# A new order for all steps of a recurrent attention with a gated layer behind it, and a table load of the sine's own

## The chip, the cores and the metric

The kernel runs on one core of one Trainium2 chip. The metric is the time of one execution on the device, in microseconds. The engines, each with its own queue of instructions, are TensorE (PE in the profile; its weight loads are PEld), VectorE (DVE), ScalarE (ACT), GpSimd (POOL) and SyncE (SP), which issues nearly all DMAs.

## The reference, cut to what matters

```python
# q, k, v, f_logit: (4, 8, 768, 48)
f = 1.0 / (1.0 + np.exp(-f_logit))
for t in range(S):
    state = f[:, :, t, :, None] * state + np.einsum('bhd,bhe->bhde', k[:, :, t], v[:, :, t])
    y[:, :, t] = np.einsum('bhd,bhde->bhe', q[:, :, t], state)
x = y.transpose(0, 2, 1, 3).reshape(3072, 384)
h = x @ w_in                    # (384, 2048)
out = (h * np.cos(h)) @ w_out   # (2048, 384)
```

## The kernel before, in words

**Chunks.** The recurrence is turned into matrix products over chunks of 128 tokens. Two chunks make a *pair* of 256 tokens; a batch has three pairs, and there are twelve, 0 to 11. Pairs 0 and 1 have their loads and gates cut in two halves (`.0` and `.1`, four heads each); the others are loaded whole.

**The steps of a pair n.** Every step has a name, and the same names are used in the order of the work.
- `f`, `k`, `q`, `v` (lines 300 to 302, on SP): the loads.
- `ex`, `ln`, `fx`, `fy` (lines 333 to 351, ScalarE): the logarithm of the gate, and the gate itself. `ad` (line 367, GpSimd) adds the logarithms of neighbouring tokens. `cum` (lines 378 and 384, TensorE) sums them along the chunk; `eb` and `ei` (lines 395 and 399, ScalarE) are the exponentials of these sums, with either sign.
- `qa`, `ka` (lines 342, 345 and 355) fold one token's gate into q and k; `qm`, `km` (line 408) multiply by the decays. They read two operands in SBUF and may be put on VectorE or GpSimd.
- `tq`, `tk` (line 439) transpose on TensorE into PSUM and `qkt` (line 198) copies the result to SBUF; for pairs 5 to 11 a DMA transpose issued by SP (line 428) does both.
- `sc` (line 462, TensorE) are the scores, `am` (line 474, VectorE) masks them.
- `vb`, `vt` (line 198, GpSimd or ScalarE) cast and rearrange v.
- `ps` (line 492, TensorE) is the product that makes the state; `st`, `sd` (lines 504 and 509, VectorE) add the state carried and decay it; `sm` (lines 517 and 519) spreads it for the next product.
- `y`, `yi` (line 545, TensorE) sum the chunk's output in PSUM; `xe` (line 198) copies it to SBUF as x.

**The steps of a unit m.** The layer behind it runs over units of tokens: two of 128, then eleven of 256.
- `h` m.js (line 612, TensorE): x times a part of w_in; two halves s fill a PSUM place of two banks. In the two narrow units such a half has twelve matmuls, otherwise six.
- `co` (line 617, ScalarE): the cosine, as the sine with pi/2 added. `g` (line 584, VectorE): the product with h.
- `o` c.s (line 634, TensorE): chunk c of 128 tokens, one fourth of w_out each; `ot` copies the sum, `out` (line 646) stores it. The last chunk, 23, is cut in two columns, `a` and `b`.

**The weights.** `w0.i` and `w1.i` (line 286) load fourths of w_in and w_out, 768 KB each, into slots that g later uses; `wc` (line 198) casts them to bf16.

**The order.** `ORDER` is a text written by a planner outside the kernel. A word as `g0.0:V2` names the step, the letter of the engine (T, S, V, G, Y for TensorE, ScalarE, VectorE, GpSimd, SP) and the slot or PSUM bank of what it makes. `emit` issues the steps in just that order, and each engine works through its own in order. The waits follow from what the steps read and write. `zf` steps (line 268) are matmuls of zeros that nobody reads; they stand where TensorE would wait in the first part. `zsp`, `zqk`, `zvt` zero the edges of buffers once.

ScalarE's functions lie in two tables here: one for the exponential and the logarithm, one for the sine. `emit` asks for the first by an instruction (line 677) where a step of it follows one of the sine's; the load of the second is put in automatically and has the line of the sine, 617.

Of the kernel before, what the change touches and what calls it, by code (L numbers as in the profile page):

```python
# [55 lines left out]
h0.11:T0 co2.1:S2 h0.10:T qa2:G h1.11:T4 h1.10:T co2.0:S0 qm2.1:G0 g2.1:V3 wc1.0:G qm2.0:G co0.1:S1  # L56
v2:Y1 co1.1:S2 g2.0:V h2.20:T6 h2.21:T co2.2:S0 h2.31:T2 h2.30:T co2.3:S3 sm1.1:S0 wc1.1:G g0.1:V
g1.1:V g2.2:V o3.0:T0 o0.0:T1 o1.0:T4 tq2.1:T5 o3.1:T tq2.0:T6 o1.1:T f3:Y1 ka2:G km2.1:G
tk2.1:T w1.3:Y4 f4:Y0 v3:Y0 zsp.1:G g2.3:V km2.0:V wc1.2:S ex3:S ln3:S0 fx3:S zqk.2:G
tk2.0:T k3:Y0 vb2:G0 o3.2:T qkt2.1:V0 sc2.1:T2 vt2.1:G0 wc1.3:S vt2.3:G ps2.1:T5 ps2.0:T k4:Y1  # L60
o1.2:T qkt2.0:V1 st2.0:V o0.1:T sc2.0:T6 vt2.0:G q4:Y0 sd2.0:V0 o0.2:T am2.1:V0 sm2.0:G1 yi2:T5,2
ex4:S ln4:S1 vt2.2:G fx4:S ad3:G1 fy4:S ad4:G2 am2.0:V1 y2:T xe2.1:V0 xe2.0:V cum3:T3
o3.3:T o0.3:T ot3:V0 ot0:V1 vb3:G0 o1.3:T h3.20:T6 cum4:T2 eb3:S0 ot1:V2 f6:Y2 ei3:S0
ka3:V km3.0:V0 h3.01:T0 ei4:S1 eb4:S1 h3.00:T h3.21:T km3.1:V ps3.0:T2,3 ps3.1:T ka4:G h3.10:T4
sd3.0:V0 st3.1:V h3.11:T sd3.1:V1 qa4:G h3.31:T2 h3.30:T co3.2:S0 g3.2:V0 o4.2:T6 km4.0:G1 q3:Y1
qm4.0:G qm4.1:G q5:Y2 co3.0:S1 o2.3:T7 f5:Y0 v4:Y0 q6:Y0 sm3.1:S0 co3.1:S2 co3.3:S0 out3:Y
out0:Y g3.0:V tk4.0:T0 g3.1:V km4.1:G fy3:S g3.3:V o4.0:T tk3.0:T1 tq4.1:T4 tq4.0:T qkt4.0:V0
# [690 lines left out]
```

## Time and profile before

| what | value |
|---|---|
| time, median of 3 runs | 178.4 us (178.3 to 178.56) |
| time of the profiled execution | 179.66 us |
| its span | 177.4 us |
| granted TensorE clock | 1.00 |
| busy: PE, DVE, ACT, POOL | 170.8, 136.0, 137.7, 100.1 us |
| a load of f, k, q or v (whole) | 384 KB |
| loads of weights | 8 of 768 KB |
| HBM read, written | 25.17 MB, 4.72 MB |

Times of the profile count from the span's start. A row of the timeline gives start, duration, engine, line, operation, the tile written and those read, the count, and, where the engine had been idle, for how long and who ended that. A table of stretches gives the busy time and the count of each engine in each stretch. In the chain of waits a row is start, duration, and the work that the end depended on. "<-DMA" means that a load's landing ended the wait.

### The profile page before, as it was taken

The numbers are of one execution on the slowest core, as the hardware profiler recorded it, in microseconds if no ns is written. First come the engines' busy times: TensorE is split into PE (matmuls) and PEld (weight loads), VectorE is DVE, ScalarE is ACT, GpSimd is POOL, SyncE is SP. The second block draws the span as 40 slices with busy tenths as digits, with TensorE's granted clock in tenths as the row PEclk, the third lists the DMA queues.
The fourth block names the chain that finished last, engine by engine and source line by source line (L and its number), as shares of the span: only waits on it lengthen the run. The fifth ranks groups of instructions, "written<-read, shape, count | busy, mean of one in ns | idle before, by whom it ended". The sixth has DMA issues, their size and how long they took to land.

```text
span 177.4 us, 5843 instructions
## 1 busy us (share of the span) xinstructions
PE 170.8 (96%) x2470; PEld 124.8 (70%) x2470; DVE 136.0 (77%) x196; ACT 137.7 (78%) x205; POOL 100.1 (56%) x128
## 2 busy tenths in 40 slices
...
GB/s 127 276 261 306 353 352 351 305 229 280 256 258 286 285 185 134 285 171 235 247 260 279 211 227 232 199 155 163 48 193 2 0 137 4 0 44 4 0 113 198
DMA packets 72281, 33.92 MB, mean 191 GB/s; under 512 B 65344, under 2 KB 70720, under 8 KB 72256
## 3 DMA queue, kind: packets, MB, share of 16 engines
...
HBM read 25.17 MB, written 4.72 MB: 168 GB/s over the span
## 4 chain that ended last, share of the span: by engine, by line
PE 75%; DMA 11%; ACT 3%; DVE 3%; SPq 2%; POOL 2%; issue 1%; DVEq 0%; POOLq 0%
PE ps L634 33%; PE ps L612 28%; DMA g<-in_moe_w_in_dram 5%; DMA v<-in_v_dram 5%; PE ps L545 4%; PE ps L462 3%; SPq L286 2%; PE ps L492 2%; PE ps L268 2%; POOL w_in_bf L198 2%; DMA f<-in_f_logit_dram 2%; PE ps L439 1%; DVE am L474 1%; PE ps L378 1%; DVE qk L408 1%
## 5 line engine op out<-in xcount | busy, mean ns | idle before, releaser
L584 DVE TENSOR_TENSOR g<-ps,co 128x1024 bf16<-128x1024 f32 x48 | 60.1, 1309 | 19.2 <-ACT co L617 16.0
L634 PE MATMUL ps<-w_out_bf,g 128*128 128x384 bf16 (+1 forms) x400 | 69.2, 320 | 0.8 <-ACT w_out_bf L198 0.8
L612 PE MATMUL ps<-x,w_in_bf 128*128 128x256 bf16 (+1 forms) x624 | 66.6, 264 | 0.5 <-POOL w_in_bf L198 0.4
L617 ACT ACTIVATE co<-ps,halfpi 128x1024 bf16<-128x1024 f32 x48 | 51.7, 1113 | 18.2 <-PE ps L612 16.3
L612 PEld LDWEIGHTS <-w_in_bf 128*128 128x128 bf16 x624 | 56.5, 98 | 8.4 <-issue 0.6
L634 PEld LDWEIGHTS <-g 128*128 128x128 bf16 x400 | 37.1, 98 | 21.0 <-issue 1.0
L474 DVE TENSOR_TENSOR am<-ps,pmask 128x1024 bf16<-128x1024 f32 x22 | 26.0, 1216 | 1.5 <-PE ps L462 1.4
L408 POOL TENSOR_TENSOR qk<-q,b 128x384 bf16<-128x384 f32 x18 | 17.8, 1003 | 3.4 <-DVE q L342 2.2
L408 POOL TENSOR_TENSOR qk<-k,bi 128x384 bf16<-128x384 f32 x16 | 16.3, 1027 | 4.8 <-issue 2.0
L198 POOL COPY vt<-vb 64x384 bf16<-64x384 bf16 x31 | 15.3, 503 | 1.4
L268 PE MATMUL ps<-zero 128*128 128x512 bf16 x44 | 13.9, 426 | 1.2 <-DVE zero L204 1.2
L198 ACT COPY ot<-ps 128x384 f32<-128x384 f32 (+1 forms) x13 | 5.9, 450 | 8.9 <-PE ps L634 7.2
L198 POOL CAST vb<-v 128x768 bf16<-128x768 f32 x9 | 7.7, 861 | 8.3 <-DMA v<-in_v_dram 8.3
L333 ACT ACTIVATE f<-f 128x768 f32<-128x768 f32 (+1 forms) x14 | 10.3, 751 | 2.5 <-DMA f<-in_f_logit_dram 2.4
L198 DVE CAST x<-ps 128x384 bf16<-128x384 f32 x16 | 8.4, 550 | 4.5 <-PE ps L545 4.4
L519 POOL TENSOR_TENSOR sz<-sd,half 128x384 bf16<-128x384 bf16 x10 | 8.2, 826 | 5.8 <-DVE sd L509 5.5
L367 POOL TENSOR_TENSOR sp<-ls 128x384 bf16<-128x384 f32 x10 | 10.0, 1001 | 2.6 <-ACT ls L337 2.3
L345 POOL TENSOR_TENSOR q<-f,q 128x384 f32<-128x384 f32 x9 | 9.3, 1037 | 1.0 <-DMA q<-in_q_dram 0.4
L355 POOL TENSOR_TENSOR k<-k,f 128x384 f32<-128x384 f32 (+1 forms) x7 | 6.8, 973 | 4.1 <-DMA k<-in_k_dram 2.0
L198 DVE COPY ot<-ps 128x384 f32<-128x384 f32 (+1 forms) x13 | 6.7, 519 | 3.2 <-PE ps L634 3.0
L462 PE MATMUL ps<-qkt 48*64 48x128 bf16 (+1 forms) x304 | 8.9, 219 | 0.1
L198 ACT COPY vt<-vb 64x384 bf16<-64x384 bf16 x17 | 8.6, 508 | 0.3
...
## 6 DMA issues: line engine op xcount, KB each, us to landing
...
```

Source lines behind the costliest of these rows:

```text
L198: (nc.scalar.copy if e == "ACT" else eng(e).tensor_copy)(out=o, in_=i)
L268: G.step(f"zf{i}", ("PE",), lambda e, dump=dump: nc.tensor.matmul(dump.ap, lhsT=zero[:, 0:128], rhs=zero, start=True, stop=True), writes=[ ...
L333: nc.scalar.activation(out=flat(t.ap), in_=flat(t.ap), func=AF.Exp, scale=-1.0)
L345: eng(e).tensor_mul(out=w.ap[:, :, 0, :], in0=t.ap[:, :, 1, :], in1=w.ap[:, :, 0, :])
L367: G.step(f"ad{n}", ("POOL",), lambda e: eng(e).tensor_add(out=sp.ap[:, 0, :, 0:D], in0=soft.ap[:, :, 0, :], in1=soft.ap[:, :, 1, :]), read ...
L408: G.step(f"{nm}{n}.{u}", ("POOL", "DVE"), lambda e, u=u, j=j, src=src, dec=dec: eng(e).tensor_mul(out=qkp[u][j].ap[:, :, :, 0:D], in0=swap ...
L462: nc.tensor.matmul(o[t, r, 2 * a + g, :].rearrange("p (e n) -> p e n", e=2), lhsT=w, rhs=qkv(u)[s, 0, a, g, :, :], start=(a == 0 and g == ...
L474: G.step(f"am{n}.{u}", ("DVE",), lambda e, u=u, sc=sc: nc.vector.tensor_mul(out=am[u].ap.rearrange("p r b n -> p (r b) n"), in0=sc.ap.rear ...
L584: nc.vector.tensor_mul(out=o.rearrange("p b (n e) -> p b e n", e=2), in0=ph.ap.rearrange("p (b e n) -> p b e n", e=2, n=64), in1=co.ap.rea ...
L612: nc.tensor.matmul(ph.ap[:, i * T:(i + 1) * T].rearrange("p (g t) -> p g t", t=C), lhsT=w_in_bf[:, kk, f0:f0 + 128], rhs=xa[:, :, kk, :], ...
L617: G.step(f"co{m}.{j}", ("ACT",), lambda e, ph=ph, co=co: nc.scalar.activation(out=co.ap, in_=ph.ap, func=AF.Sin, bias=halfpi), reads=[ph], ...
L634: nc.tensor.matmul(po.ap[:, 0:c1 - c0], lhsT=gap[:, j, i * C:(i + 1) * C], rhs=w_out_bf[:, j, c0:c1], start=(po.first and j == 4 * s), sto ...
```

## The change: what it does

It changes three things.

1. `ORDER` is another text. All steps of pairs and units are the same, but their order, the engine of some, and the slots differ. Steps by engine, before and after: `ka` 7 on VectorE and 7 on GpSimd, then 3 and 11; `km` 8 and 16, then 6 and 18; `qm` 6 and 18, then 2 and 22; `qa` 5 and 9, then 4 and 10. `vt`: 31 on GpSimd and 17 on ScalarE, then 28 and 20. `wc`: 5 and 3, then 6 and 2. `xe`: 16 on VectorE and 8 on ScalarE, then 13 and 11. `ot`: 13 and 13, then 11 and 15. `qkt`: 9 and 1, then 8 and 2. `sm`: one moves from GpSimd to VectorE. Two stores, `out22.1` and `out23.0`, are issued by ScalarE.
2. The matmuls of zeros are 41 and no longer 44 (the width of each could now be set; all are 512 as before).
3. `emit` asks for the sine's table by an instruction too.

New code that cuts the loads and casts of w_in in halves is there, but `CUT_LOAD` and `CUT_CAST` are empty, so it does nothing; `SC8` isn't used.

The diff, with the order cut to the words around the first use of the weights:

```diff
+CUT_LOAD = ()
+CUT_CAST = ()
+SC8 = 1
-ZEROS = 44
+ZEROS = (512,) * 41
 ORDER = """
-zsp.2:G zvt.0:V f0.0:Y0 f0.1:Y ex0.0:S q0.1:Y0 k0.0:Y0 zqk.1:G q0.0:Y f1.1:Y1 ln0.0:S2 ex0.1:S
...
-q2:Y0 w1.0:Y4 qkt1.0:V1 ex2:S ln2:S0 xe0.1:S wc0.0:S zf39:T2 sc1.0:T4 zf40:T2 zf41:T2 yi1:T6,2
-ad2:G2 zf42:T3 zf43:T3 cum2:T3 vt1.1:G am1.1:V0 vt1.0:G fy2:S h0.00:T0 wc0.1:G am1.0:V1 w1.1:Y0
-fx2:S eb2:S0 y1:T st1.1:V xe1.0:V1 ei2:S1 xe1.1:S k2:Y1 sd1.1:V1 h1.00:T4 h2.00:T2 w1.2:Y1
-h0.01:T h1.01:T h2.11:T6 wc0.3:G zqk.0:G co0.0:S0 wc0.2:G g0.0:V2 h2.01:T h2.10:T co1.0:S1 g1.0:V
...
+zsp.1:G zqk.1:G f0.1:Y0 f0.0:Y ex0.1:S ex0.0:S ln0.1:S1 ln0.0:S q0.0:Y0 fx0.0:S qa0.0:V zvt.0:V
...
+ps1.0:T7,3 zf35:T4 tq1.1:T w0.3:Y3 xe0.1:S qkt1.1:V0 sd0.1:V0 ps1.1:T st1.0:V qm1.0:G ad2:G1 zf36:T4
+zf37:T4 zf38:T4 zf39:T4 tq1.0:T sc1.1:T0 sd1.0:V1 wc0.0:S k2:Y0 qkt1.0:S1 zf40:T4 cum2:T2 ei2:S1
+h1.00:T4 am1.1:V0 st1.1:V sc1.0:T0 am1.0:V1 sd1.1:V2 sm1.0:S0 eb2:S0 sm0.1:G1 wc0.1:G q2:Y1 vt1.3:G
+zqk.0:V h0.00:T6 h0.01:T co0.0:S0 w1.1:Y4 w1.3:Y1 y1:T0,1 v2:Y1 wc0.2:G w1.2:Y2 f4:Y1 yi1:T
+xe1.1:S1 h1.01:T xe1.0:V h0.10:T2 sm1.1:V0 co1.0:S1 h2.20:T0 g0.0:V0 wc0.3:G g1.0:V h2.21:T h0.11:T
+co2.2:S2 co0.1:S1 h1.10:T6 ka2:G km2.0:G0 qa2:G zsp.0:V qm2.1:G km2.1:G h1.11:T g2.2:V3 co1.1:S0
+g0.1:V h2.00:T4 g1.1:V h2.01:T co2.0:S2 h2.10:T0 h2.11:T wc1.1:S qm2.0:G h2.31:T2 tk2.1:T6 h2.30:T
+f3:Y0 g2.0:V tk2.0:T7 tq2.1:T qkt2.1:V0 co2.1:S0 o0.1:T4 tq2.0:T co2.3:S1 w1.0:Y4 wc1.3:G g2.1:V
+vb2:G0 vt2.1:G0 vt2.3:G vt2.2:G k3:Y0 o1.1:T5 g2.3:V qkt2.0:S1 o0.3:T o1.3:T sc2.0:T0 am2.0:V0
+sc2.1:T6 v3:Y0 ps2.1:T2 ps2.0:T st2.0:V sd2.0:V0 o3.3:T3 wc1.2:G ex4:S ln4:S0 vt2.0:G o3.1:T
+o1.2:T o0.2:T ex3:S ln3:S1 sm2.0:G1 yi2:T2,0 q4:Y0 am2.1:V1 y2:T xe2.1:V0 k4:Y1 v4:Y1
+ad4:G0 f6:Y2 cum4:T1 xe2.0:S o3.2:T ad3:G1 q3:Y1 fy3:S eb4:S0 ei4:S0 wc1.0:G h3.31:T6
+fx3:S fy4:S h3.30:T cum3:T2 eb3:S1 ei3:S1 ka3:V h3.21:T0 fx4:S km3.0:V0 vb3:S0 o0.0:T
+co3.3:S0 o1.0:T o3.0:T ot0:V0 ps3.0:T2,4 km3.1:G ps3.1:T ot3:V1 sd3.0:V0 qa4:G qm4.1:G1 st3.1:V
...
+co7.3:S1 g6.0:V g7.1:V g7.3:V cum9:T2 eb9:S1 vt9.0:S1 ka9:G vt7.2:G o11.1:T3 o12.2:T6 o11.0:T
+ei9:S0 o12.0:T o11.2:T sc7.1:T0 tq8.1:Y2 qm8.0:G zqk.2:V ps8.1:T7 am7.1:V0 sc7.0:T4 tq8.0:Y3 ex11:S
+vt8.3:S ex10:S am7.0:V1 vt8.1:G ln11:S0 vt7.3:S o12.3:T o10.2:T2 o12.1:T ps8.0:T st8.0:V sc8.0:T0
+am8.0:V2 sc8.1:T4 sd8.0:V0 ot12:S1 sm7.0:S2 vt8.2:G km9.0:G0 am8.1:V3 km9.1:G o10.1:T o11.3:T o10.0:T
+ot11:S2 ln10:S1 qm9.0:G y7:T0,1 sm8.0:G3 yi7:T ad10:G0 yi8:T3,4 y8:T fy11:S xe7.0:S0 xe8.0:S1
+xe8.1:V ps9.0:T0,5 ps9.1:T vt9.2:S out8:Y tq9.0:Y4 sc9.0:T6 o10.3:T xe7.1:V zsp.2:V sd9.0:V0 ot10:V0
...
 """
-        if s.table is not None:
-            if s.table == "E" and table != "E":
-                nc.scalar.preload_act_table_set("natural_log_exp_and_others")
+        if s.table is not None and s.table != table:
+            nc.scalar.preload_act_table_set({"E": "natural_log_exp_and_others", "S": "trig_and_small"}[s.table])
             table = s.table
```

More of the change, by code (lines that the diff above doesn't have):

```diff
@@ L56 @@
[L56 to L67, printed above, removed]
@@ L92 @@
-vt9.2:G vt8.2:G g6.0:V o12.0:T4 o10.1:T5 o12.3:T cum9:T0 o12.2:T ei9:S1 km9.0:G2 eb9:S1 qm9.0:G
-qm9.1:G km9.1:G vt7.1:G o12.1:T ps8.0:T0 ps8.1:T sc7.1:T6 st8.0:V sc8.0:T2 ex11:S sm7.1:S1 am8.0:V0
-sd8.0:V0 am7.1:V1 ot12:S1 tq7.0:Y2 o13.2:T1 o13.0:T ex10:S o13.1:T ln11:S0 o13.3:T fy11:S tq8.1:Y3
-out7:Y q10:Y0 sc7.0:T2 am7.0:V2 ps9.1:T0,4 vt8.1:G sc8.1:T6 ps9.0:T q11:Y1 am8.1:V3 ln10:S1 fy10:S
-sm8.0:S3 v11:Y0 k10:Y0 o10.3:T o10.2:T sd9.0:V0 ot13:V0 yi7:T2,3 y7:T xe7.1:S0 fx10:S vt8.0:G
-yi8:T6,7 vb10:G2 out12:Y ad10:G0 y8:T st9.1:V xe7.0:V ad11:G1 vt10.0:G1 cum10:T0 eb10:S0 sd9.1:V1
@@ new lines @@
+ot11:S2 ln10:S1 qm9.0:G y7:T0,1 sm8.0:G3 yi7:T ad10:G0 yi8:T3,4 y8:T fy11:S xe7.0:S0 xe8.0:S1
+xe8.1:V ps9.0:T0,5 ps9.1:T vt9.2:S out8:Y tq9.0:Y4 sc9.0:T6 o10.3:T xe7.1:V zsp.2:V sd9.0:V0 ot10:V0
+st9.1:V cum10:T4 sd9.1:V1 k11:Y0 k10:Y1 fx10:S ei10:S0 out6:Y am9.0:V0 fx11:S eb10:S0 h8.31:T0
+h8.21:T2 h8.30:T h8.20:T vt9.3:G qm9.1:G tq9.1:Y0 ad11:G1 o13.3:T4 o13.2:T o13.1:T o13.0:T co8.2:S0
+co8.3:S1 ot13:S3 fy10:S v11:Y0 q10:Y0 out13:Y vb10:G1 vt9.1:G g8.2:V1 ka10:G h8.00:T6 km10.0:G1
+km10.1:G sm9.1:S0 g8.3:V vb11:G0 ps10.1:T2,3 ps10.0:T sc9.1:T4 h8.01:T out12:Y vt10.2:S0 co8.0:S0 st10.0:V
```

149 lines of the change are left out of this document (78 added, 71 removed).

## The prediction

> **What bounds the kernel now.** I read the page's busy times and slices first, then a table of stretches, then the chain of waits, then the timeline of the stage that looked unlike the rest.
>
> ```profile
> PE 170.8 (96%) x2470; PEld 124.8 (70%) x2470; DVE 136.0 (77%) x196; ACT 137.7 (78%) x205; POOL 100.1 (56%) x128
> ...
> core 0: us, PE busy (x) PEld busy (x) DVE busy (x) ACT busy (x) POOL busy (x), PEclk, DMA share, GB/s
> 1.20:21.30 20.10, 19.52 (x269) 10.29 (x269) 15.88 (x46) 16.50 (x36) 8.37 (x15) 1.00 1.09 275
> 21.30:46.10 24.80, 23.31 (x333) 17.64 (x334) 18.30 (x22) 21.21 (x26) 19.19 (x22) 1.00 1.06 303
> 46.10:54.00 7.90, 7.73 (x98) 6.12 (x96) 7.11 (x11) 7.66 (x12) 6.75 (x8) 1.00 1.11 258
> 54.00:127.00 73.00, 72.98 (x1211) 55.86 (x1209) 65.61 (x89) 68.77 (x103) 62.66 (x78) 1.00 1.02 214
> 127.00:174.30 47.30, 47.28 (x567) 34.87 (x565) 28.79 (x30) 22.81 (x31) 2.57 (x4) 1.00 0.21 59
> 174.30:177.40 3.10, 0.00 (x0) 0.00 (x0) 0.00 (x0) 0.32 (x1) 0.00 (x0) 1.00 0.42 131
> ```
>
> From 54 us to 174.3 TensorE is never idle, at clock 1.00. The matmuls are the same in both kernels, so an order can win nothing there; it can only lose. The tail after the last matmul is 3.1 us. What is left is the head, where the DMA engines are full (share 1.06 and 1.09): up to 21.3 us TensorE waits for the first quarter of w_in and burns zero matmuls, and from 21.3 to 46.1 it is fed as weights arrive.
>
> Busy 23.31 of 24.80 flatters that second stage, since each step's modelled end hides some waiting. So I count its work, at rates from steps that run without a wait:
>
> ```profile
> 22.66 4.80 PE L612 MATMUL ps<-x,w_in_bf 128*128 128x128 bf16 x60
> ...
> 58.61 0.22 PE ps L439 x4
> 61.01 0.37 PE ps L492 x32
> 61.93 0.27 PE ps L378
> 66.10 10.49 PE ps L612 x96
> 111.07 1.68 PE ps L545 x112
> 121.87 0.57 PE ps L462 x32
> 159.92 1.30 PE ps L634 x8
> ```
>
> An h step of six 256-wide matmuls is 6 x 10.49/96 = 0.655 us; one of twelve 128-wide ones is about 0.65 (the x60 row is 36 narrow and 24 wide ones: 4.80 less 24 x 0.109, over three). An o step is 0.65, a tk or tq 0.22, y plus yi 0.84 (56 of the x112 row), a cum about 0.35 (its wide matmul 0.27, four small ones), a two-part sc or ps under 0.3. The stage from the first w_in matmul (21.33) to h3.20 (46.11) holds 8 narrow and 8 wide h steps 10.4, y1 0.5, twelve o 7.8, tk2/tq2 0.9, sc2 and ps2 0.9, y2 with yi2 0.84, cum3 0.35: 21.7 us of work in 24.8. **So 3.1 us are lost there**, and that is nearly all that can be won.
>
> **The change part by part.** First what sets the stage:
>
> ```profile
> 21.33 0.84 PE L612 MATMUL ps<-x,w_in_bf 128*128 128x128 bf16 x12
> 21.99 1.46 POOL L198 CAST w_in_bf<-g 128x1536 bf16<-128x1536 f32 x1 [0.26 <-DMA g<-in_moe_w_in_dram]
> 24.26 1.47 POOL L198 CAST w_in_bf<-g 128x1536 bf16<-128x1536 f32 x1 [0.80 <-DMA g<-in_moe_w_in_dram]
> 26.38 1.47 POOL L198 CAST w_in_bf<-g 128x1536 bf16<-128x1536 f32 x1 [0.18 <-DMA g<-in_moe_w_in_dram]
> 26.48 9.71 DVE L584 TENSOR_TENSOR g<-ps,co 128x1024 bf16<-128x1024 f32 x8 [3.10 <-POOL qk L234]
> 31.14 1.46 POOL L198 CAST w_out_bf<-g 128x1536 bf16<-128x1536 f32 x1 [1.16 <-DMA g<-in_moe_w_out_dram]
> 36.08 1.35 DVE L408 TENSOR_TENSOR qk<-k,bi 128x384 bf16<-128x384 f32 x1
> 37.19 1.47 ACT L198 CAST w_out_bf<-g 128x1536 bf16<-128x1536 f32 x1 [2.03 <-DMA v<-in_v_dram]
> 38.18 0.82 POOL L198 CAST vb<-v 128x768 bf16<-128x768 f32 x1 [0.46 <-DMA v<-in_v_dram]
> 40.93 2.35 DVE L474 TENSOR_TENSOR am<-ps,pmask 128x1024 bf16<-128x1024 f32 x2
> 46.11 0.82 PE L612 MATMUL ps<-x,w_in_bf 128*128 128x256 bf16 x6
> ```
>
> A cast that waits for its DMA starts when the weight lands: quarters of w_in 2.1 to 2.3 us apart, w1.0 at 31.1, w1.2 at 37.2, v2 at 38.2.
>
> *Up to the first w_in matmul.* The new SP order has before w0.0 the same nine loads of 384 KB as the old one (f, k, q, v of pairs 0 and 1, and f2), only shuffled, so w0.0 lands when it did. Its cast is again ACT's next instruction after xe0.1. The first w_in matmul stays at 21.3. The three zeros fewer (44 to 41) are therefore worth nothing: they filled a wait. Yet yi1 (0.36) and sc1.0 (0.25), done before 21.3 in the old order, come after it now. That costs 0.6.
>
> *From 21.3 on, the new order against its gates.* The fed work is h1.00, sc1.0, h0.00, until 22.85; h0.01 needs w0.1, cast at 21.99 + 1.46 = 23.45: 0.6 lost. Then h0.01, y1, yi1, h1.01 to 25.6. h0.10 needs the third quarter: 24.26 + 1.47 = 25.73; to 26.4. h2.20 needs xe1.1, on ACT behind the table load and co0.0, 26.6; two steps to 27.9. h0.11 needs the last quarter, 26.38 + 1.47 = 27.85. Nine h steps and three transposes run through to 34.4. The order now asks first for w1.1, which comes after k2 and q2 where w1.0 came after q2 alone: 384 KB later. That load costs between 1.0 (w1.2 to v2) and 2.5 us (last quarter to w1.0, 4.76, less 2.2 for w1.0 itself); I take 1.2, near the first, since weights and inputs alternate here as they do there. So w1.1 lands at 32.3; ACT casts it behind co2.0 by 33.8, in time. o0.1, tq2.0, o1.1 to 35.9; o0.3 and o1.3 need w1.3 (34.5 and a cast, 36.0), to 37.3; sc2, ps2 to 38.2; o3.3, o3.1 to 39.5. w1.2 lands at 38.4, POOL casts it to 39.9: 0.4 lost; o1.2, o0.2 to 41.2.
>
> Next is POOL's queue, with these prices:
>
> ```profile
> L367 POOL TENSOR_TENSOR sp<-ls 128x384 bf16<-128x384 f32 x10 | 10.0, 1001 | 2.6 <-ACT ls L337 2.3
> L198 POOL COPY vt<-vb 64x384 bf16<-64x384 bf16 x31 | 15.3, 503 | 1.4
> L519 POOL TENSOR_TENSOR sz<-sd,half 128x384 bf16<-128x384 bf16 x10 | 8.2, 826 | 5.8 <-DVE sd L509 5.5
> L408 POOL TENSOR_TENSOR qk<-q,b 128x384 bf16<-128x384 f32 x18 | 17.8, 1003 | 3.4 <-DVE q L342 2.2
> ```
>
> vt2.0 and sm2.0 follow that cast: 39.9 + 0.5 + 0.83 = 41.2, when yi2 wants it. yi2, y2 to 42.05, cum4, o3.2, two h3 steps, cum3 and h3.21 to 45.5. Last comes o0.0, which needs w1.0: f4, f3 and itself after w1.2, 38.4 + 2.5 + 2.2 = 43.1, cast on POOL to 44.7. In time.
>
> VectorE would have been late for this pace in the old order: eight gates from 26.48, the 1.35 us km2.0, two copies, two am, until 43.28, and y2 waited for that. In the new one km2.0 is on POOL and a copy on ACT, some 2 us off that row of work; its am2.1 ends near 41.
>
> *The sum of the stage.* By 46.11 the old order has 21.7 us done, 22.3 with yi1 and sc1.0. By 45.5 the new one has 16 narrow and wide h steps 10.4, three h3 2.0, y and yi of two pairs 1.7, sc1.0 0.25, tk2/tq2 0.9, nine o 5.85, sc2 and ps2 0.9, two cum 0.7: 22.7. Ahead by 0.6 of time and 0.4 of work: **1.0 us**.
>
> *The shared port.* km3.1 in the old order and its like show what a meeting costs:
>
> ```profile
> 7.08 0.56 DVE L408 TENSOR_TENSOR qk<-k,bi 128x384 bf16<-128x384 f32 x1
> ...
> 47.69 1.83 DVE L408 TENSOR_TENSOR qk<-k,bi 128x384 bf16<-128x384 f32 x2
> 47.91 1.20 POOL L355 TENSOR_TENSOR k<-k,f 128x384 f32<-128x384 f32 x1 [0.74 <-ACT bi L399]
> ```
>
> Alone such a VectorE product takes 0.56; the pair that met ka4 on POOL took 1.83, 0.7 too much, and POOL's 1.0 became 1.20. The new order moves eleven ka, km, qm and qa steps from VectorE to POOL, so most meetings go; outside the head only TensorE's spare time is touched. One stays on the path: km3.0 (VectorE) and km3.1 (POOL) become ready together near 46, just ahead of ps3. VectorE first costs nothing; POOL first holds up km3.0, two ot copies and the sd3 that free banks for h3, by up to 0.75. I take 0.2.
>
> The Trainium skill says in "SBUF — State Buffer", under "SBUF: two separate sides", that the pair of ports is an exclusive lock held for a whole instruction, by whichever starts first. The 1.83 and 1.20 rows agree roughly: both sides lose. By that rule with POOL first the sum would be 0.55 us worse than mine.
>
> *The rest.* The moved steps cost POOL eleven times 1.0 and one weight cast more 1.5; three vt, one sm and some memsets fewer give back about 3. POOL goes from 100 to some 109 us, in a stretch (54 to 127) where it had 10.3 idle. ACT gains nine small copies (vt, xe, ot, a qkt) of about 0.5 and loses one cast of 1.5: some 3 us, and it had 4.2 idle there, with more after 127. Both are covered by TensorE's queue if the order of it fits; if not, see the rivals. The table load moves little:
>
> ```profile
> L617 ACT ACT_TABLE_LOAD x6 | 7.7, 1283 | 0.7 <-issue 0.6
> 124.31 1.28 ACT L617 ACT_TABLE_LOAD   x1 [0.65 <-issue]
> ```
>
> Six loads of the sine already start early; one waited 0.65 us, beside a busy TensorE. The new order has the same six switches each way. The two output issues on ACT, near the end, fall where ACT idles. The tail stays 3.1.
>
> The sum: 1.0 - 0.2 = 0.8 off the profiled execution's span of 177.4 (179.66 with what lies around it), so 176.6; off the median 178.4, **177.6 us**. 0.36 us (0.2%) is about what can be told from no change.
>
> **The rivals.** *The gain is eaten in the head*: 178.4. POOL now casts w1.3, w1.2 and w1.0 between its other work; from 39.9 on everything behind yi2 has no slack. If the 384 KB load costs 2.5 rather than 1.2, w1.1 makes o0.1 0.7 late and w1.2's cast 1.3 late. For it: only 0.5 us lies between my times and the gates. Against: after 21.3 the old order lost 3.1, so it takes several.
>
> *Slower: the DMA transposes of pair 9 come late.* In the new order sc9.0 follows h7.30 closely: between them eleven o 7.15, four sc 1.1, ps8 0.37, y7, y8 and their yi 1.7, cum9 and ps9 1.1, 11.4 us. The other way round goes co7.3 1.1 and 0.2 latency, table load 1.28, eb9 0.48, a vt 0.5, ei9 0.48, then POOL's km9.0, km9.1, qm9.0 3.0, then the transpose:
>
> ```profile
> DMA to landing us min/median/max: 3.1/4.5/6.8
> ```
>
> 7.1 + 4.5 = 11.6 is level with 11.4; the longest, 6.8, makes TensorE 2.5 us late: 177.6 + 2.5 = 180.1; at 5.1 and more the kernel is slower than before. Against: no input load is issued just ahead of tq9.0 now, so it should be one of the short ones.
>
> *The set named for the sine isn't the one that the automatic load wants*: six more loads, 7.7 us of ACT, against 4.2 idle between 54 and 127, where five of them would fall (6.4): 2.2 late, 179.8. Against: the exponential's set is named in the same way, and no second load shows beside it.
>
> **How the numbers follow.** Forecast 0.54 (its own range 176.8 to 178.0); eaten gain 0.20; late transposes 0.22 (spread from 178.8 to 180.1); second load 0.04. Faster 0.54, within 0.2% 0.20, slower 0.26. If the whole 3.1 lost came back the time would be near 176; the weights' landings exclude most of it, so the low end is 176.6; the high end takes in most of the late transposes, 179.4.
>
> **What would show it.** In the profile after: the first w_in matmul at 21.3; o0.0 of L634 near 45.5 without a wait for POOL's w_out cast; am2.1 done near 41; no VectorE product over 1 us; 12 table loads; TensorE without idle from 54 on; its last end near 173.5. I am wrong if the first w_in matmul is more than 0.5 off, if a wait over 0.5 us for POOL stands on TensorE between 39 and 50, or if TensorE idles before L462 after 60 us.

## The result, and the profile after

The changed kernel takes 184.2 us (median of 4 runs, 183.57 to 184.92); the kernel before takes 178.48 beside it (178.3 to 179.74). The ratio is 1.031, with a 95% interval from 1.024 to 1.037. The forecast was 177.6, with a range up to 179.4. The profiled execution took 184.47 us, its span is 182.7. Where a kernel has a slow run beside its fast ones (three runs of e6 below, and one of the kernel before at 287.68 us), the ratios here are of the fast runs alone.

The table of stretches of the kernel after (stretch; length, then the busy time and count of each engine, TensorE's clock, DMA share, GB/s), under the page's line of busy times:

```profile
PE 171.4 (94%) x2464; PEld 125.3 (69%) x2467; DVE 131.8 (72%) x181; ACT 140.7 (77%) x213; POOL 109.4 (60%) x135
...
core 0: us, PE busy (x) PEld busy (x) DVE busy (x) ACT busy (x) POOL busy (x), PEclk, DMA share, GB/s
21.30:46.10 24.80, 24.67 (x396) 19.87 (x394) 20.31 (x26) 22.72 (x31) 21.62 (x22) 1.00 1.12 310
...
54.00:76.00 22.00, 22.00 (x337) 17.42 (x335) 18.32 (x24) 21.58 (x33) 20.54 (x26) 1.00 0.97 250
76.00:96.00 20.00, 17.92 (x346) 12.08 (x344) 13.26 (x21) 16.16 (x28) 18.45 (x25) 1.00 1.05 208
96.00:120.00 24.00, 22.85 (x396) 17.35 (x394) 18.64 (x23) 21.05 (x31) 19.16 (x23) 1.00 0.82 167
120.00:142.00 22.00, 20.54 (x244) 15.28 (x241) 19.08 (x18) 18.31 (x25) 13.22 (x16) 1.00 0.49 107
```

The same view of the kernel before, for the last three of these stretches:

```profile
76.00:96.00 20.00, 20.00 (x369) 14.28 (x367) 17.36 (x29) 19.17 (x32) 15.91 (x22) 1.00 1.04 241
96.00:120.00 24.00, 24.00 (x395) 18.44 (x393) 20.96 (x26) 21.81 (x31) 21.69 (x28) 1.00 1.12 207
120.00:142.00 22.00, 21.98 (x331) 16.23 (x330) 20.04 (x24) 14.66 (x22) 8.51 (x11) 1.00 0.39 82
```

From 21.3 to 76 us TensorE (PE) of the kernel after is as full as before, or fuller. Then it idles 2.08, 1.15 and 1.46 us in three stretches where before it idled next to nothing. Its last matmul ends 5.4 us later (179.71 against 174.29); the tail is 3.0 us, as forecast. What it waited for, in the whole span (engine, line, releaser: total, times, longest):

```profile
PE ps L623 <- issue: 2.6, 2, 1.4
PE ps L623 <- DVE g L595: 1.4, 2, 1.1
...
PE ps L473 <- DMA qkt<-qk: 0.3, 1, 0.3
PE ps L389 <- POOL sp L378: 0.3, 1, 0.3
```

What is left out lies ahead of 21 us. The rows shown lie after 76, and the timeline shows where. The first is two waits with no releaser, "issue":

```profile
89.85 0.69 PE L556 MATMUL ps<-qkt,sz 128*32 128x128 bf16 x36
90.36 1.06 PE L556 MATMUL ps<-am,vt 128*32 128x128 bf16 x64
91.36 0.44 PE L503 MATMUL ps<-vb,qk 64*64 64x48 bf16 x32
91.73 2.47 PE L623 MATMUL ps<-x,w_in_bf 128*128 128x256 bf16 x21
95.63 1.59 PE L623 MATMUL ps<-x,w_in_bf 128*128 128x256 bf16 x13 [1.44 <-issue]
...
112.93 0.63 PE L556 MATMUL ps<-am,vt 128*32 128x128 bf16 x32
113.39 0.84 PE L556 MATMUL ps<-qkt,sz 128*32 128x128 bf16 x48
...
116.16 1.36 PE L623 MATMUL ps<-x,w_in_bf 128*128 128x256 bf16 x11
118.67 1.59 PE L623 MATMUL ps<-x,w_in_bf 128*128 128x256 bf16 x13 [1.15 <-issue]
```

Both stand in the middle of an h step: TensorE had everything the step needs and still stopped, for 1.6 and 1.3 us counted from start to start of the matmuls. Both follow a cluster of small matmuls (yi5, yi6, y6, y5, ps7.0, ps7.1; y7, yi7, yi8, y8, ps9.0, ps9.1, sc9.0). The second wait, in the timelines of VectorE (DVE), GpSimd (POOL) and TensorE:

```profile
133.88 5.03 DVE L419 TENSOR_TENSOR qk<-k,bi 128x384 bf16<-128x384 f32 x2 [1.03 <-DMA out_dram<-ot]
138.84 3.66 DVE L595 TENSOR_TENSOR g<-ps,co 128x1024 bf16<-128x1024 f32 x3
...
133.85 1.00 POOL L356 TENSOR_TENSOR q<-f,q 128x384 f32<-128x384 f32 x1 [5.35 <-ACT bi L410]
134.79 0.83 POOL L201 COPY vt<-vb 64x384 bf16<-64x384 bf16 x1
135.59 2.91 POOL L419 TENSOR_TENSOR qk<-q,b 128x384 bf16<-128x384 f32 x3
...
140.18 0.82 PE L623 MATMUL ps<-x,w_in_bf 128*128 128x256 bf16 x6 [1.08 <-DVE g L595]
141.37 0.81 PE L623 MATMUL ps<-x,w_in_bf 128*128 128x256 bf16 x6 [0.37 <-DVE g L595]
```

km11.0 and km11.1 take 5.03 us on VectorE; undisturbed they take 1.03 (in e2, below). They end 0.41 us behind the last of three products that GpSimd ran without a gap (135.59 + 2.91 = 138.50). Behind them wait g10.1 and g9.0, whose PSUM banks h10.01 and h10.30 need: 1.8 us from start to start.

So the account of the 5.4 us is: 0.35 ahead at 76 us (there both kernels have done the same 124 steps, at 76.08 and 76.43); 0.8 lost at sc5.1 and cum8 (85 to 87), 1.6 at 94, 1.3 at 117, 1.8 at 139 to 141. That leaves 0.3 in small pieces.

Three theories for the experiments. **T1**: TensorE runs out of instructions. Its program reaches it in pieces, by a DMA queue of its own. The view of the queues, then that view for 93.0 to 94.3 us and for 116.4 to 117.5 (queue: packets, MB, share), and then the table of stretches: up to the end of the first stop, from there to the end of the second, and from the second cluster's start to there:

```profile
q8 instruction: 19, 0.31, 0.7%
...
q8 instruction: 1, 0.02, 5.9%
...
q8 instruction: 1, 0.02, 5.5%
```

```profile
0.00:95.62 95.62, 89.93 (x1370) 64.30 (x1373) 71.18 (x118) 85.08 (x135) 76.63 (x97) 0.98 1.04 260
95.62:118.66 23.04, 21.89 (x384) 16.48 (x384) 19.02 (x23) 20.76 (x31) 18.55 (x23) 1.00 0.84 168
...
112.92:118.66 5.74, 4.60 (x181) 3.68 (x180) 4.16 (x9) 5.30 (x10) 5.01 (x7) 1.00 1.12 209
```

19 packets for 2,467 weight loads and as many matmuls are some 260 instructions a piece (0.31 MB / 19 is 16 KB). Between the two stops lie 384 matmuls and 384 weight loads, exactly 3 x 256. From 89.85 to the first stop 36 + 64 + 32 + 21 = 153 matmuls run; so the piece that was used up, 128 of them with their weight loads, had begun with the 26th, near 90.2, and lasted 3.7 us. From 112.92 to the second stop it is 180; that piece had begun near 113.7, among the 48, and lasted 3.6 us. In each of the two short windows just one piece was fetched. Cut finer, the same view puts these fetches at 93.05 to 94.27 and at 116.46 to 117.42: they began 2.8 to 2.9 us after the piece then in use had begun, and TensorE went on some 1.3 us after they had ended. **T2**: VectorE lost the shared port to GpSimd over and over. **T3**: the head gave less than the 1.0 forecast since the granted clock fell while TensorE waited at 13.4 to 15.5. The rivals to these were the DMA transposes that SP issued at the same moments (93.1 and 116.4), a GpSimd that is late by itself, and weights that come when they come.

### The profile page after: what moved, and what is told of

Same layout as the page of the kernel before. It is cut to its first block, busy times and chain, and to the rows that moved or that the text cites. A ratio compares the mean times of both kernels' runs of the same rounds, so it can differ in the third digit from the quotient of the medians.

```text
span 182.7 us, 5836 instructions
## 1 busy us (share of the span) xinstructions
PE 171.4 (94%) x2464; PEld 125.3 (69%) x2467; DVE 131.8 (72%) x181; ACT 140.7 (77%) x213; POOL 109.4 (60%) x135
## 5 line engine op out<-in xcount | busy, mean ns | idle before, releaser
L623 PE MATMUL ps<-x,w_in_bf 128*128 128x256 bf16 (+1 forms) x624 | 68.3, 264 | 4.0 <-issue 2.6
L595 DVE TENSOR_TENSOR g<-ps,co 128x1024 bf16<-128x1024 f32 x48 | 60.0, 1306 | 15.4 <-ACT co L628 15.4
L628 ACT ACTIVATE co<-ps,halfpi 128x1024 bf16<-128x1024 f32 x48 | 51.7, 1115 | 19.6 <-PE ps L623 13.5
L419 POOL TENSOR_TENSOR qk<-q,b 128x384 bf16<-128x384 f32 x22 | 22.0, 1003 | 2.3 <-DVE q L353 1.6
L419 POOL TENSOR_TENSOR qk<-k,bi 128x384 bf16<-128x384 f32 x18 | 18.4, 1036 | 7.5 <-ACT bi L406 5.1
L687 ACT ACT_TABLE_LOAD x12 | 15.4, 1283 | 0.9 <-PEq L752 0.7
L201 ACT COPY ot<-ps 128x384 f32<-128x384 f32 (+1 forms) x15 | 6.7, 446 | 10.6 <-PE ps L645 9.2
L270 PE MATMUL ps<-zero 128*128 128x512 bf16 x38 | 12.9, 472 | 1.6 <-DVE zero L207 1.2
L201 DVE CAST x<-ps 128x384 bf16<-128x384 f32 x13 | 6.9, 552 | 6.7 <-PE ps L556 6.7
L366 POOL TENSOR_TENSOR k<-k,f 128x384 f32<-128x384 f32 (+1 forms) x11 | 10.5, 956 | 1.9 <-DMA k<-in_k_dram 1.6
L530 POOL TENSOR_TENSOR sz<-sd,half 128x384 bf16<-128x384 bf16 x9 | 7.4, 828 | 5.2 <-DVE sd L520 3.0
L201 ACT COPY vt<-vb 64x384 bf16<-64x384 bf16 x20 | 10.2, 508 | 0.3
L201 DVE COPY ot<-ps 128x384 f32<-128x384 f32 (+1 forms) x11 | 5.8, 536 | 5.9 <-PE ps L645 5.9
```

The lines of the kernel that those rows point to most:

```text
L201: (nc.scalar.copy if e == "ACT" else eng(e).tensor_copy)(out=o, in_=i)
L270: G.step(f"zf{i}", ("PE",), lambda e, dump=dump, w=w: nc.tensor.matmul(dump.ap[:, 0:w], lhsT=zero[:, 0:128], rhs=zero[:, 0:w], start=True, ...
L366: eng(e).tensor_mul(out=w.ap[:, :, 0, :], in0=w.ap[:, :, 0, :], in1=t.ap[:, :, 0, :])
L419: G.step(f"{nm}{n}.{u}", ("POOL", "DVE"), lambda e, u=u, j=j, src=src, dec=dec: eng(e).tensor_mul(out=qkp[u][j].ap[:, :, :, 0:D], in0=swap ...
L595: nc.vector.tensor_mul(out=o.rearrange("p b (n e) -> p b e n", e=2), in0=ph.ap.rearrange("p (b e n) -> p b e n", e=2, n=64), in1=co.ap.rea ...
L623: nc.tensor.matmul(ph.ap[:, i * T:(i + 1) * T].rearrange("p (g t) -> p g t", t=C), lhsT=w_in_bf[:, kk, f0:f0 + 128], rhs=xa[:, :, kk, :], ...
```

## The experiments

All times are medians; the kernel before took 178.8 in each of the three sets.

### e2: only the edges of the pieces moved

```diff
-ZEROS = (512,) * 41
+ZEROS = (96,) * 19 + (512,) * 22 + (96,) * 82
```

The 82 new zero matmuls stand behind zf9 and zf18, so that nearly the same columns of zeros come before the first real work (9,696 for 9,728).

> The kernel after with its first 19 matmuls of zeros (512 columns) cut into 101 of 96 columns: the same columns, but 164 more instructions in TensorE's stream ahead of all the work; nothing else is touched. Theory (TensorE runs out of instructions): the trace moves TensorE's instructions in pieces of 256 (2,467 pairs of weight load and matmul in 19 pieces), and both waits with no releaser (1.6 us at 94.0, 1.3 us at 117.4) stand 768 instructions apart, each right where a piece of 256 ends that was used up within 4.1 and 4.4 us because a cluster of small matmuls filled it. With the pieces' edges 164 instructions earlier, the two clusters straddle an edge; both waits are gone, PE's row for issue at L623 falls from 2.6 us to under 0.4, and the time is 181.0 to 181.8. Rival (the DMA transposes tq7.1 and tq9.1, issued at 93.1 and 116.4, hold TensorE or its fetch up): these are where they were, the waits stay, 184.2.

Measured: 180.16 us (179.81 to 180.61), ratio to before 1.008 (1.005 to 1.010): 4 us off, more than expected. TensorE's waits after 60 us, in the view of waits:

```profile
PE ps L393 <- POOL sp L382: 0.7, 1, 0.7
PE ps L507 <- POOL qk L423: 0.4, 1, 0.4
```

No "issue" is left, and none for g. The h steps behind the first cluster are now one row (line numbers are 4 higher):

```profile
91.86 5.41 PE L627 MATMUL ps<-x,w_in_bf 128*128 128x256 bf16 x48
```

164 instructions that compute nothing, 85 us earlier, took both stops away: T1 as expected, and the transpose tq7.1 was issued at 93.2 as it was before. The piece in use where the first cluster begins now started at 85.7, and lasted 5.2 us; the fetch of the next ended 2.3 us before TensorE came to it. The queue of instructions has 20 pieces here. The excess is T2's: with the stops gone, km11.0 and km11.1 came at another moment and took 0.56 us each (551 to 559 ns in the view of that tile).

### e3: the transposes later

```diff
-out2:Y tq7.1:Y0 xe6.1:V
+out2:Y xe6.1:V
...
-f11:Y2 h6.10:T2
+f11:Y2 tq7.1:Y0 h6.10:T2
...
-qm9.1:G tq9.1:Y0 ad11:G1
+qm9.1:G ad11:G1
...
-v11:Y0 q10:Y0 out13:Y
+v11:Y0 q10:Y0 tq9.1:Y0 out13:Y
```

> The kernel after with tq7.1 behind the loads f10 and f11, and tq9.1 behind v11 and q10 in SP's order. Theory (TensorE runs out of instructions by itself): the two waits at 94.0 and 117.4 stay at 1.6 and 1.3 us within 0.3, and the time at 184.2 within 0.4. Rival (the transposes that are issued at the same moment hold up TensorE or the fetch of its instructions): both waits are gone, 181.2 to 181.8.

Measured: 182.43 us (181.79 to 183.54). The view of waits, and the row behind the first stop:

```profile
PE ps L623 <- issue: 3.1, 2, 1.8
...
95.46 1.26 PE L623 MATMUL ps<-x,w_in_bf 128*128 128x256 bf16 x10 [1.83 <-issue]
```

The stops stayed, the first at 2.0 and the second at 1.5 us from start to start, though the first transpose was now issued at 96.7: it is not their cause. Yet the time fell by 1.8, which neither side had expected. km11.1 took 1.35 us here (both together 1.83), and there is no wait for g. So e3 moved the other loss, without meaning to.

### e12: the clusters thinned

```diff
-sm5.0:S2 o6.0:T o6.1:T out7:Y
+sm5.0:S2 out7:Y
...
-yi5:T0,1 yi6:T2 y6:T3
+yi5:T0,1 yi6:T2 o6.0:T y6:T3 o6.1:T
...
-o11.3:T o10.0:T
+o11.3:T
...
-yi7:T ad10:G0 yi8:T3,4 y8:T
+yi7:T o10.0:T ad10:G0 yi8:T3,4 o10.3:T y8:T
...
-sc9.0:T6 o10.3:T xe7.1:V
+sc9.0:T6 xe7.1:V
```

> The kernel after with four w_out steps of 0.65 us put between the small matmuls: o6.0 and o6.1 into the cluster yi5 to y5, o10.0 and o10.3 into the cluster y7 to y8; the number of instructions stays. Theory (a piece of 256 instructions used up in 4 us is the cause): with 1.3 us of long matmuls in each piece the fetch is in time, both waits with no releaser are gone, 181.0 to 181.8, and 179.5 to 180.3 if the shift of 2.9 us also spares km11.1 its meeting, as in the run with the cut zeros. Rival (what matters is only where the edges of the pieces lie, not how fast they are used): the waits stay, 184.2.

Measured: 181.32 us (180.82 to 181.54), ratio 1.013 (1.008 to 1.018). The stops are gone here too, and the h steps behind the first cluster are one row:

```profile
92.16 6.09 PE L623 MATMUL ps<-x,w_in_bf 128*128 128x256 bf16 x53
```

The number of instructions is the same, and so nearly are the edges; what changed is how fast a piece is used up. At the first cluster the fetch began as late as with the stops, 2.8 us after the piece in use, but that piece now lasted 5.3 us, and TensorE went on 1.6 us after the fetch had ended. With e2 this settles T1: an edge at the start of a cluster, and nothing long in the cluster, were both needed here. They are not enough by themselves. Counted on in steps of 128 weight loads, the piece that begins near 151 us in the kernel after and that at 109.3 in e2 are used up in 3.6 and 3.8 us without a stop; there the fetch of the next piece had begun at most 0.9 us after the piece itself. What makes a fetch begin late no run shows. km11 was spared as well (1.02 for both), but of that gain a part went to waits at sc6.0, sc5.1, cum8 and h8.31 (0.2, 0.5, 0.3 and 0.4).

### e6: the kernel before, with the edges moved

```diff
-ZEROS = 44
+ZEROS = 60
```

The first three zero matmuls and the sixteen new ones behind zf7 have 80 columns, the others 512 as before.

> The kernel before, with three of its zero matmuls cut into 19 of 80 columns at the same place, so 32 more instructions ahead of all the work and nothing else. Theory (TensorE runs out of instructions where a cluster of small matmuls begins at the edge of a piece of 256): with this shift a piece of the kernel before begins at yi7 at 111.0 and would be used up in 3.7 us, and one at 143.1 in 3.8; in the kernel after the pieces used in 4.1 and 4.4 us cost 1.6 and 1.3. So the kernel before gets waits with no releaser near 114.7 and perhaps 146.9, and is 1.3 to 3.5 us slower, 179.8 to 182. Rival (the waits belong to something in the order after, its DMAs or semaphores at these places): 178.5 within 0.4.

Measured: ten runs from 178.61 to 183.3, median 180.94; the kernel before lay between 177.94 and 179.93. The ratio, of the seven runs up to 181.15, is 1.008 (1.003 to 1.012). Three of these seven are 180.9 or more, which no run of before reaches; four are 180.0 or less. So the shift made this kernel slower in a part of its executions, by some 2 us, as T1 expects. The profiled one is one of the four, and even it has a stop, 0.5 us from start to start:

```profile
91.52 1.69 PE L612 MATMUL ps<-x,w_in_bf 128*128 128x256 bf16 x14 [0.34 <-issue]
```

It stands behind 1,373 weight loads, just as the first stop of the kernel after does (the first stretch above), and the piece ahead of it was used up in 4.2 us. At 114.7, where the stop had been expected, there is none: that piece was used up in 3.3 us, but the fetch of the next had begun only 0.9 us after the piece itself. What the slower executions lost no trace shows.

### e1: km11 on GpSimd

```diff
-km11.0:V0 km11.1:V
+km11.0:G0 km11.1:G
```

> The kernel after with km11.0 and km11.1 on GpSimd, ahead of qa11, instead of on VectorE. Theory (VectorE was locked out of the shared port): km11.1 took 3.73 us on VectorE at 135.2 to 138.9 while five GpSimd rows ran without a gap, and TensorE's waits of 1.24 and 0.53 us for g10.1 and g9.0 at 138.8 to 141.4 come from it. On GpSimd both take 1.0, g10.1 ends near 138 instead of 140.1, the two waits are gone, and the time is 182.2 to 182.8 (184.2 less 1.4 to 2.0). Rival (GpSimd is late by itself, since it had waited 5.4 us for ei11, and whatever comes behind is late): with two more rows on GpSimd the waits stay or turn up at the transposes of pair 11, and the time is 184 or more.

Measured: 183.13 us (182.12 to 183.55), 1.1 less than the kernel after. The row of km11 on GpSimd, and VectorE's g steps behind it, from the timeline:

```profile
135.00 1.96 POOL L419 TENSOR_TENSOR qk<-k,bi 128x384 bf16<-128x384 f32 x2 [5.44 <-ACT bi L410]
...
137.77 3.71 DVE L595 TENSOR_TENSOR g<-ps,co 128x1024 bf16<-128x1024 f32 x3 [3.85 <-ACT co L628]
```

km11 took 1.0 each, the g steps now wait for ScalarE's cosine, and TensorE doesn't wait for them. T2's place is right; a GpSimd with 2 us more to do wasn't missed. The gain fell short of 1.4; in the traced execution the two stops were longer (3.0 us together against 2.6), and small waits at cum8 and an sc had grown by some 0.6, which would account for it.

### e10: the kernel after once more

No edit.

> The kernel after once more, not changed. Theory (VectorE's km11.1 meets GpSimd's run of products in this order each time): km11.1 takes over 2 us again, TensorE waits again at h10.01 and h10.30, 183.6 to 185. Rival (the 3.7 us were an accident of one execution): km11.1 takes 0.56 to 1.4 us, no wait at h10.01, 182.2 to 182.9 as in the run with later transposes. The two waits with no releaser near 94 and 117 come in both.

Measured: 184.33 us (184.31, 182.52, 184.36, 184.38). The view of that tile on VectorE from 133 to 139 us (minimum, median, maximum in ns):

```profile
L419 DVE TENSOR_TENSOR qk<-k,bi x2: 739/2234/3728, 134.4 to 135.1; 128x384 bf16<-128x384 f32 x2
```

km11.1 took 3,728 ns; in the first trace it was 3,730. So in both traces it asked during the copy vt11.0 (134.67 to 135.50 here), and waited for all three products behind it. In e3 it asked during qa11 and came through 0.41 after that row's end. One of the four runs, 182.52, is 1.8 shorter, and no trace shows why; since the kernel after thus lies between 182.52 and 184.92 over both sets, what e1 and e3 show rests on their traces more than on their medians. The two stops are in all four traces that keep TensorE's order up to here (the kernel after, e10, e3, e1), each time behind 1,373 and 1,757 weight loads, with fetches that began 2.7 to 3.1 us after the piece in use and ended 1.25 to 1.6 us before TensorE went on.

### e7 and e11: the port by itself

Rows added behind the kernel's end: in e7 equal products on both engines, in e11 on GpSimd the sequence of qa11, vt11.0 and three products, seven times.

```diff
+pstart:V pg0:G pg1:G pg2:G
...
+pc0:V pv0:V pv1:V pv2:V pv3:V pc1:V pc2:V pv4:V
```

```diff
+pstart:V pa0:G pt0:G pg00:G pg01:G pg02:G pa1:G
...
+pv0:V pv1:V pc0:V pc1:V pc2:V pv2:V pv3:V
```

`pg` and `pv` are the products on GpSimd and VectorE, `pa` and `pt` the product in F32 and the copy, `pc` copies from PSUM.

> The kernel after with rows added behind its end that compute nothing of it: 30 products like qm and km (half as many elements as nothing is cut: 128x8x48) on GpSimd without a gap, and meanwhile 12 of the same on VectorE, four back to back and the others with copies from PSUM between them. Its time means nothing (about 30 us more). Theory (VectorE, asking while GpSimd has the next product queued, is sometimes passed over): the products on VectorE, 0.56 alone, spread from 0.6 to over 2.4 us, and the long ones end 0.41 after the end of a GpSimd row. Rival (the port goes over at the end of the row that holds it, and km11.1 was a single accident of another kind): none over 1.4 us, that is one GpSimd row of 1.0 and 0.41.

> The kernel after with rows added behind its end that compute nothing of it: seven times on GpSimd the sequence that met km11.1 (a product in F32 like qa11, a copy of 64 partitions like vt11.0, three products like qm), and on VectorE seven pairs of products back to back with three or four copies from PSUM between, so that they meet it at different places; half as many elements are not taken, sizes are those of the real rows (128x384 and 64x384). Its time means nothing. With equal products alone no row on VectorE took over 1.36 us. Theory (it is the copy of 64 partitions that lets VectorE ask at a bad moment and be passed over by the products behind it): one of the pairs has a row of over 2.4 us whose end lies 0.41 behind a GpSimd row's end. Rival (the port always goes over at the end of the row that holds it; something else held km11.1): none over 1.5 us.

The products on VectorE in e7:

```profile
L669 DVE TENSOR_TENSOR pov<-pa,pb x12: 772/1228/1362, 181.0 to 198.1; 128x384 bf16<-128x384 f32 x12
```

None over 1.36: the rival held, and with products against products VectorE had the port at the end of the row that held it. In e11 the longest are 1.70:

```profile
191.94 0.84 POOL L201 COPY pvt<-pvb 64x384 bf16<-64x384 bf16 x1
192.74 3.33 POOL L670 TENSOR_TENSOR pog<-pa,pb 128x384 bf16<-128x384 f32 x3
...
192.44 1.70 DVE L670 TENSOR_TENSOR pov<-pa,pb 128x384 bf16<-128x384 f32 x1
```

Two products asked during the copy (192.44 and 197.46), both took 1.70 and ended 0.41 behind the first product that followed. So neither forecast held (over 2.4, none over 1.5), and T2 is borne out in part: one that asks during GpSimd's copy is passed over by the next product, but here by one, not by three. In e11 the products lie 0.08 us apart (3.33 for three against 2.91), and in the kernel after they overlap. Whether that difference makes it three wasn't tried.

### e4: zeros against the idle stretch

```diff
-sm0.0:S0 y0.0:T4
+zf123:T7 zf124:T7 zf125:T7 zf126:T7 zf127:T7 zf128:T7 zf129:T7 zf130:T7 sm0.0:S0 y0.0:T4
```

(on top of e2)

> The kernel with the cut zeros, and eight more matmuls of 512 zero columns in TensorE's idle time ahead of y0.0 (13.5 to 15.4). Theory (the granted clock fell to half at 14.2 to 18.6 since TensorE idled there, so zeros and transposes took 0.43 us each and the first w_in matmul came at 22.5 instead of 21.3): the clock stays up, h1.00 begins at 21.6 to 21.9, and the time is 0.5 to 0.9 under that of the kernel with the cut zeros alone. Rival (the first w_in matmul waits for the cast of w0.0, which ends at 21.7, and for VectorE's queue; the clock of the filler is worth nothing): h1.00 at 22.3 or later, the time the same within 0.2.

Measured: 183.21 us (182.8 to 183.92), 3.1 worse than e2. The experiment missed its aim:

```profile
16.09 2.51 PE L274 MATMUL ps<-zero 128*128 128x512 bf16 x8 [1.89 <-DVE am L483]
```

The fillers waited themselves for VectorE's am0.10, whose scores lie in the other bank of the same PSUM tile, and then stood in front of y0.0. h1.00 began at 24.99. Nothing about the clock follows.

### e5 and e9: all repairs together

In e5, against the kernel after:

```diff
-ZEROS = (512,) * 41
+ZEROS = (56,) * 10 + (512,) * 31 + (56,) * 82
...
-vt1.2:S0 vt1.0:S w0.2:Y2 qa1.0:V st0.1:V vt1.1:S
+vt1.2:S0 w0.2:Y2 qa1.0:V st0.1:V
-w0.3:Y3 xe0.1:S qkt1.1:V0
+w0.3:Y3 wc0.0:S xe0.1:S vt1.0:S vt1.1:S qkt1.1:V0
-tq1.0:T sc1.1:T0 sd1.0:V1 wc0.0:S
+tq1.0:T zf40:T4 h1.00:T4 sc1.1:T0 sd1.0:V1
...
-ot7:V3 cum8:T6
+ot7:V3
-o6.3:T7 o6.2:T
+o6.3:T7 cum8:T6 o6.2:T
...
-ps10.1:T2,3 ps10.0:T sc9.1:T4 h8.01:T
+sc9.1:T4 h8.01:T ps10.1:T2,3 ps10.0:T
```

In e9, against e2:

```diff
-ka7:G ad8:G0 fx8:S
+ad8:G0 ka7:G fx8:S
...
-ps10.1:T2,3 ps10.0:T sc9.1:T4 h8.01:T
+sc9.1:T4 h8.01:T ps10.1:T2,3 ps10.0:T
```

> The kernel after with four edits. (1) As before, 164 more instructions from cut zeros, but all in the idle stretch ahead of cum0.0 (the first ten zeros become 92 of 56 columns), since in the run with the cut zeros the first transpose and with it the load of w0.0 came 0.5 us later. (2) The cast of w0.0 on ScalarE ahead of xe0.1, vt1.0 and vt1.1, and h1.00 ahead of sc1.1 and cum2 on TensorE. (3) cum8 behind o6.3, (4) ps10.1 and ps10.0 behind sc9.1 and h8.01, since in the run with the cut zeros TensorE waited 0.72 us at cum8 for ad8 and 0.69 us at ps10.1 for km10.1. Theory (each of these waits lies on TensorE's path): 180.2 less 0.5 less 0.9 less 1.0, so 177.4 to 178.2, h1.00 at 21.3 to 21.6. Rival (the head is set by the arrival of the nine weight loads, whatever TensorE does first): only the 1.0 of the edits 3 and 4, 179.0 to 179.6.

> The kernel with the cut zeros (180.2), and two steps moved where its TensorE still waited: ad8 ahead of ka7 on GpSimd (cum8 waited 0.72 us for it), and ps10.1, ps10.0 behind sc9.1 and h8.01 on TensorE (0.69 us for km10.1). Theory (these are the last waits on TensorE's path outside the head): both gone, 180.2 less 1.4 is 178.8, within 0.4, no faster than the kernel before. Rival (a step made later lets the next be late, as cum8 behind o6.3 did): 179.6 or more, with a wait at a later sc or h.

Measured: e5 181.41 (180.54 to 182.52), e9 181.06 (179.85 to 181.29). Neither is better than e2. In e5 the first w_in matmul did come 1.6 us earlier than in e2, and the gain was gone 3 us later, and again before 46:

```profile
21.14 0.83 PE L623 MATMUL ps<-x,w_in_bf 128*128 128x128 bf16 x12 [0.38 <-ACT x L201]
...
23.68 0.40 PE L473 MATMUL ps<-qkt 48*128 48x128 bf16 x8 [1.04 <-DVE am L485]
...
106.71 0.42 PE L473 MATMUL ps<-qkt 48*64 48x128 bf16 x16 [0.67 <-DMA qkt<-qk]
...
111.01 0.64 PE L473 MATMUL ps<-qkt 48*64 48x128 bf16 x32 [1.59 <-DMA qkt<-qk]
```

sc1.0, at 23.68 as in e2, waited for VectorE; o0.0 began at 46.51, in e2 at 46.44. So the first w_in matmul doesn't set the head by itself. At sc7.0 and sc8.0 TensorE then waited for the transposes of pairs 7 and 8; cum8, whose exponentials these need, had been made one o step later, but that this is the cause was not tried alone. In e9, with ad8 ahead of ka7, the wait at cum8 is gone and 0.6 us each stand at sc6.0 and sc8.0. So e9's rival held; e5 came out slower than either side had it. In this order the steps of the pairs have little slack, and a wait that is mended at one place is followed by another.

### e8: the table load alone

```diff
-            if s.table == "E" and table != "E":
-                nc.scalar.preload_act_table_set("natural_log_exp_and_others")
+            if s.table != table:
+                nc.scalar.preload_act_table_set({"E": "natural_log_exp_and_others", "S": "trig_and_small"}[s.table])
```

(in the kernel before)

> The kernel before with the sine's table loaded by an instruction of its own, the change's smallest part alone. Theory (the load stands at the same place in ScalarE's queue, 12 loads of 1.28 us as before): 178.5, the same within 0.3. Rival (the load of its own comes earlier, beside other work, or is done twice): 0.5 or more to either side.

Measured: 178.62 us (178.35 to 179.39), ratio 0.999 (0.996 to 1.001). Worth nothing, as expected.

### The clock in the head

The run made for T3, e4, missed its aim, but the first 84 us of the order are the same in the kernel after, in e10 and in e12. The stretch from 13.5 to 19 us, in the kernel after:

```profile
13.50:19.00 5.50, 3.69 (x60) 2.02 (x53) 4.78 (x9) 5.46 (x13) 3.73 (x7) 0.74 1.10 320
```

in e10:

```profile
13.50:19.00 5.50, 3.57 (x60) 2.18 (x49) 4.34 (x9) 5.46 (x13) 3.73 (x7) 0.69 1.10 314
```

and in e12:

```profile
13.50:19.00 5.50, 3.75 (x101) 2.39 (x94) 4.26 (x10) 5.46 (x13) 3.73 (x7) 1.00 1.09 315
```

At a granted clock of 0.74 and 0.69, 60 matmuls ran in these 5.5 us; at 1.00, 101. h1.00 began at 22.51, 22.45 and 21.69, o0.0 at 46.12, 46.56 and 45.36, and the 124 steps that the kernel before has done at 76.43 were done at 76.08, 76.50 and 75.35. In e1 and e3, whose edits come later too, the clock was 0.69 and 0.76, and this point was reached at 76.08 and 75.83. So in the one of these five executions that kept the clock up the head gained 1.08, in the four that lost it 0.6 to nothing. That the clock is the cause, and why it fell in some and not in others, was not tried. At the end of the kernel the gain doesn't show: two of e10's runs had the clock up for their whole length and took 184.36 and 184.38, the traced one, at 0.991 on average, 184.31.

## Why the prediction was wrong

- **"From 54 us to 174.3 TensorE is never idle ... an order can win nothing there; it can only lose."** Right, and all of the loss lies there. The prediction then priced this stretch with one rival and two sentences on what is covered.
- **"Both are covered by TensorE's queue if the order of it fits."** The busy times came as forecast (POOL 109.4 for some 109, ACT 140.7 for 137.7 + 3), but the cover failed in three places. The largest, 2.9 us, was no engine's lateness at all: the prediction had no term for TensorE's own supply of instructions. The kernel before holds the signs of it: its view of the queues has the same 19 pieces, and the order after sets six and seven small steps in a row where before it was four and five. The page "Runtime: NRT & Kernel Launch" of the Trainium skill, section "Instruction fetch mechanics", says that instructions come in blocks of 256, the next fetched while the current one executes, and calls the cost of crossing "mostly hidden". The first half agrees with the 768 instructions between the stops and with the fetches at 93.05 and 116.46, while the piece before was in use; the second doesn't hold here, where a piece used up in 3.6 to 3.7 us, with a fetch that began late, left TensorE waiting 1.3 and 1.6.
- **"The shared port: ... most meetings go; outside the head only TensorE's spare time is touched."** Most meetings did go, and the one expected in the head, km3, cost VectorE nothing. But a single one left over, km11.1, took 3.73 us where the longest row of before is 1.36, and it stood ahead of two g steps that TensorE needed: 1.8 us. The step that failed is the price of a meeting (0.7 to 0.75 from the rows of ka4 and km3.1) taken as its upper bound. The rule of the Trainium skill cited there, in "SBUF — State Buffer", section "SBUF: two separate sides", an exclusive lock for a whole instruction, agrees with e7, where no product of VectorE took over 1.36; it doesn't say who is next, and with a copy and three products queued VectorE waited for all of them.
- **The walk through the head, "1.0 us".** With the clock kept up, time and size came as forecast: o0.0 at 45.36 in e12 for 45.5, 1.08 ahead at 76 us. In the kernel after it was 0.35. The step that failed is "the first w_in matmul stays at 21.3": it came at 22.51, by the prediction's own test more than 0.5 off. At full clock it is still 21.7, since the cast ends then. "The three zeros fewer are therefore worth nothing" left out the clock; but that the number of zeros decides it isn't shown. Two figures of the walk were off without harm. A narrow h step is 0.73 by the working given (4.80 less 2.62, over three) and not 0.65, so that 2.5 and not 3.1 us were lost in the stage; both orders have eight of them. And w1.2 at 38.4 doesn't follow from the prices named, 34.5 + 1.2 + 2.2 = 37.9; its cast began at 37.82, without a wait. am2.1 ended at 41.9 for 41, without cost, and there was no wait of TensorE for POOL between 39 and 50.
- **The rivals.** Pair 9's transposes were in time: sc9.0 ran at 114.89 without a wait. It was pair 5's that were late, by 0.3, with cum8 behind them 0.8 in all; e5 and e9 have more waits of that kind, at pairs 7 and 8: the danger was real, the pair was another. "The gain is eaten in the head" happened in part, 0.35 left of 1.0, but not by POOL's casts, for which TensorE didn't wait; the clock is the likely cause. A second table load didn't come: 12 loads, 15.4 us, as forecast, and e8 shows the change's third part to be worth nothing.
- **The sum.** Forecast 0.8 faster. Measured on TensorE: 0.35 faster in the head, then 2.9, 1.8 and 0.8 slower and 0.3 in small pieces, 5.4. The tail of 3.1 was 3.0.

No version here beats the kernel before; the best, e2, is 0.8% slower. What it still lacks are 0.7 us at cum8, 0.4 at ps10.1 (0.7 from start to start), and the head's gain (o0.0 at 46.44, although its clock stayed at 1.00, for its load of w0.0 was issued 0.5 later).
